# Squares of odd chunks issued ahead of the x rows, pairs written a chunk sooner, and P ahead of the turning of k and q, in an mLSTM cell followed by a squared-ReLU network

## The chip, the cores and the metric

One NeuronCore of a Trainium2 chip runs the whole kernel in one launch. The metric is the device time of an execution in microseconds (us). The kernel before was timed in three runs: 490.64, 492.65 and 494.86 us, median 492.65 us. One more execution was profiled; every duration below comes from that one.

## The reference

Inputs are q, k, v and an output gate of shape (4 batches, 8 heads, 768 steps, 40), an input and a forget gate of shape (4, 8, 768), and two weight matrices. All is float32.

```
for t in range(S):                        # each batch and head
    m_new = max(f[t] + m, i[t])
    C = exp(f[t] + m - m_new) * C + exp(i[t] - m_new) * outer(v[t], k[t])
    n = exp(f[t] + m - m_new) * n + exp(i[t] - m_new) * k[t]
    y[t] = sigmoid(o[t]) * (C @ q[t]) / max(|n . q[t]|, 1)
x = y as (3072 tokens, 320)
out = max(x @ w_in, 0)**2 @ w_out         # w_in 320x2048, w_out 2048x320
```

## The kernel before

**Tiling.** The recurrence is computed in chunks of 128 steps. There are 24 chunks (6 for each batch, all heads at once), numbered s from 0 to 23. Inside a chunk the outputs are a masked matrix product of q, k and v, as in attention: `scores` multiplies k by q on TensorE into PSUM, `weighted` (line 592, VectorE) multiplies the scores by the decay weights W and gives P, and `attend_begin` and `attend_end` (lines 697 to 736, TensorE) multiply P by v, the carried state C by q (line 703), and form the next state. The network works on groups g of two chunks (256 tokens). Its first product is `ffn1_open`, `ffn1_rows` and `ffn1_close` (lines 1036 and 1085), its second one `ffn2_fast` (line 960); both are cut up so that fewer block products are needed, at the price of sums on VectorE and GpSimd (`sums`, `sums_of_x`).

**Order.** No scheduler places the work: every engine and every queue runs its instructions in the order in which the program writes them. From chunk 6 on, one loop (line 1314) walks through parts n = 0, 1, 2, ...; four parts, numbered by `at` = 0 to 3, belong to a chunk s = 6 + n // 4. In each part there is a quarter of a network product, which fills TensorE, and around it a step of the recurrence for chunk s or s + 1. From chunk 8 on, even chunks run beside a second product (`ffn2_fast`), odd chunks beside a first product (`fast` is true).

**How k and q get to TensorE.** From chunk 7 on, k and q are not transposed by TensorE. They pass through DRAM. `pair_up(s)` (line 344) copies the chunk's k and q from the inputs to a scratch tensor kq_rows, in four DMAs, from chunk 10 on issued by GpSimd. `load_squares(s)` (line 399) brings them from there into the tile kqT in four DMAs, issued by SyncE, as 32x32 squares. `turn_kq(s)` (line 406) turns every square on VectorE. The tile kqT has two buffers, so all odd chunks share one. The buffer's last readers are `scores(s)` and `scale_q(s)` (line 667, VectorE). For an odd chunk s + 1 the turning and the scores are both done in the loop's passes of the even chunk s: the turning at `at` = 0, the scores at `at` = 1, `scale_q` and `weighted` at `at` = 2.

**What SyncE's queue carries.** SyncE issues these DMAs, in this order, for a chunk s: at `at` = 1 `store_num` (line 768; the outputs, turned in squares by VectorE at line 753, to DRAM), `load_num` (line 773; back, after the store has landed), `load_squares(s + 2)`, and for an even chunk `load_A(s + 2)` (line 430); at `at` = 2 `store_rows` (line 823; the normalised x to DRAM), for an odd chunk `load_A(s + 2)`, then `load_o(s + 5)` (line 414) and `load_rows` (line 828; x back, after its store has landed). Stores of the result (lines 996 and 1001) stand between them. The x rows of an even chunk s are turned by `turn_squares(s)` (line 835, VectorE) in the pass of chunk s + 1 at `at` = 1; right behind it on VectorE stands the sum of line 1068, for which the closing product of `ffn1_close` waits[...].

**What GpSimd carries.** Besides the DMAs of `pair_up` and `load` (k and v of a chunk, lines 364 to 376) it does the mask (line 470), the weighting of v (line 521), the decay of C (line 672), and the sums of x for the network (lines 1028 and 1031).

Of the kernel before, what the change touches and what calls it, by code (L numbers as in the profile page):

```python
# [29 lines left out]
def kernel(  # L30
# [308 lines left out]
    def pair_up(s):  # L339
        b, c = divmod(s, NB)  # L340
        eng = nc.sync if s < 10 else nc.gpsimd
        for n, src in enumerate((k, q)):
            for i in range(2):
                eng.dma_start(
                    kq_d[s, i, n].rearrange("j (m r) d -> m j (r d)", r=8),
                    src[b, i::2, c * P : (c + 1) * P, :].rearrange("j (m r) d -> m j (r d)", r=8),
                )
# [68 lines left out]
    def half_tanh(s):  # L416
        og = st[s]["og"]
        nc.scalar.activation(og, og, AF.Tanh, scale=0.5)
        if s >= X_SQ:
            nc.scalar.activation(og, og, AF.Copy, bias=0.5, scale=0.5)  # L420
# [128 lines left out]
    def scores(s, o=(False, False)):  # L549
        d = st[s]  # L550

        sc = [bank(o[i]) for i in range(2)]
        d["sc"] = sc
        if s >= KQ_SQ:
            if s >= ROT:
                d["sc"] = [t.rearrange("p j t -> p (j t)")[:, : 3 * P].rearrange("p (e t) -> p e t", e=2) for t in sc]
            for e in range(2):
                for late_keys in range(2):
                    for c in range(2):
                        for i in range(2):  # L560
                            rows = slice(DP * i, DP * i + D)
                            start = e == late_keys == 0
                            if s < ROT:
                                j, keys = 2 * late_keys + e, HALVES[c]
                                to, t0 = sc[i][HALVES[c], j, :], 0
                            else:
                                j, keys = 2 * (c ^ late_keys) + e, HALVES[late_keys]
                                to = d["sc"][i][HALVES[c], e, slice(0, DP) if late_keys else slice(DP, 3 * DP)]
                                t0 = DP * late_keys
                            nc.tensor.matmul(  # L570
                                to, lhsT=d["kT"][rows, j, keys], rhs=d["qT"][rows, j, t0:], start=start, stop=True,
                                skip_group_check=True,
                            )
            return
        for j in range(PR):
            for i in range(2):
                rows = slice(DP * i, DP * i + D)
                nc.tensor.matmul(
                    sc[i][:, j, :], lhsT=d["kT"][rows, j, :], rhs=d["qT"][rows, j, :], start=True, stop=True,
                )  # L580
# [349 lines left out]
    def sums_of_weights(i):  # L930
        if i < 3:
            T[i] = late.tile([P, NPAIR, DH], F32, name=f"T{i}", bufs=1)[:]
        if i == 0:
            nc.vector.tensor_tensor(T[0], B12, B11, op=ALU.subtract)
        elif i == 1:
            nc.vector.tensor_tensor(T[1], B22, T[0], op=ALU.subtract)
        elif i == 2:
            nc.vector.tensor_tensor(T[2], B21, T[1], op=ALU.subtract)
        else:

            nc.vector.tensor_tensor(B12, B22, B12, op=ALU.subtract)
# [131 lines left out]
    def ffn1_rows(g, q, first):  # L1073
        xT, xs = st["xT", g], st["xs"]
        X, Y, V, Z = st["f1"]
        lo, hi = HALVES
        pairs = (
            ((X, lo, xT[lo, 0, 2, :], False), (Y, hi, xT[hi, 1, 2, :], first)),
            ((V, lo, xT[lo, 1, 2, :], first), (Z, hi, xs[hi, 1, :], False)),
        )  # L1080
        for pair in pairs:
            for n in range(4):
                for cols in HALVES:
                    for to, rows, rhs, start in pair:
                        nc.tensor.matmul(  # L1085
                            to[cols, n, :], lhsT=w_in2[rows, 4 * q + n, cols], rhs=rhs,
                            start=(start and n == 0), stop=True, skip_group_check=True,
                        )
# [35 lines left out]
    def do(f, s):  # L1124
        if 0 <= s < NT:
            f(s)
# [98 lines left out]
    for u in range(8):  # L1225
        s = 2 + u // 2
# [87 lines left out]
    for n, (which, g, i) in enumerate(parts):  # L1314
        s, at = 6 + n // 4, n % 4
        if n == 5:
            brought.close()
            late = ctx.enter_context(tc.tile_pool(name="late", bufs=1, side="right"))
        even = s >= 8 and s % 2 == 0
        fast = which == 1  # L1320
        if at == 0:
            if s < 8 or even:
                do(scores, s)
            if even:
                do(turn_kq, s + 1)
            if s < 8 or even:
                do(weighted, s)
        if at == 1:
            do(attend_begin, s)
            if even:  # L1330
                do(lambda s: scores(s, ("h", "h")), s + 1)
            if fast:
                ffn1_rows(g, 0, True)
            do(attend_end, s)
            do(decays, s + 1)
            do(mask, s + 1)
            if n > 4 and not even and not fast:
                do(turn_kq, s + 1)
            do(decay_C, s + 1)
            if s > X_SQ and not fast and not even:  # L1340
                do(turn_squares, s - 1)
            do(store_num, s)
            do(load_num, s)
            do(load_squares, s + 2)
            if even:
                do(load_A, s + 2)
        if 5 <= n < 8:
            sums_of_weights(n - 5)
        if n == 6:
            sums(1, slice(0, NPAIR), (1, 2))  # L1350
        if n == 8:
            sums_of_weights(3)
            sums(1, slice(0, NPAIR), (3,))
        if n == 9:
            sums(1, slice(0, NPAIR), (4,))
        if which == 2 and i == 3 and g == NG - 2:
            sums(g + 1, slice(0, NPAIR), (2,))
        if which == 2 and g > 1 and i < 2:
            sums(g, slice(0, NPAIR), (3 + i,))
        if n == 0:  # L1360
            ffn1_begin(g)
            sums_of_x(g)
            sums_of_win(2)
        if at == 3 and s >= 8 and s % 2 == 0 and s // 2 - 1 < NG:
            sums_of_x(s // 2 - 1)
        if at == 2 and not fast:
            if even:
                do(turn_squares, s - 1)
            if n > 4:
                do(scale_q, s + 1)  # L1370
        if at == 3:
            if s % 4 == 3:
                for r in range(s + 1, min(s + 5, NT)):
                    half_tanh(r)
        if fast:
            if i % 2:
                ffn1_close(g, i // 2, i == 1)
                if at == 1 and g > 2:
                    do(turn_kq, s + 1)
                    do(turn_squares, s - 1)  # L1380
            else:
                ffn1_open(g, i // 2)
                if i == 0 and g > 2:
                    sums(g - 1, slice(0, NPAIR), (2,))
            if at == 2 and g > 2:
                do(scale_q, s + 1)
        elif g == 0:
            ffn2(g, *divmod(i, 2))
        else:
            ffn2_fast(g, i)  # L1390
        if at == 2:
            do(lambda s: weigh(s, masked=True), s + 1)
            ffn1_square()
            if n < 4:
                do(turn_kq, s + 1)
                do(scale_q, s + 1)
            if even:
                do(weighted, s + 1)
            do(normalise_turned, s)
            do(store_rows, s)  # L1400
            if not even:
                do(load_A, s + 2)
            if s > 6:
                do(load_o, s + 5)
            do(load_rows, s)
            if s == 6:
                do(pair_up, s + 3)
        if s > 6 and at == (3 if even else 2):
            do(pair_up, s + 3)
        if s > 6 and at == 3:  # L1410
            if s == 7:
                load(s + 3)
            do(load, s + 4)
        if n == 3:
            turn_halves()
        if n in (9, 25):
            spread_slots(2 + n // 25)
        if at == 0:
            ffn1_square()
        if n < 5:  # L1420
            while rounding.done < LAST[n]:
                rounding.step()
# [30 lines left out]
```

## Time and profile before

| what | value |
|---|---|
| median of three runs | 492.65 us (490.64 to 494.86) |
| the profiled execution's own time | 499.0 us |
| its span, first to last instruction | 497.2 us |
| TensorE busy | 488.1 us (98% of the span), 6167 matmuls |
| VectorE, ScalarE, GpSimd busy | 336.3, 240.8, 222.0 us |
| mean granted TensorE clock | 0.990 |
| DMA traffic | 68.02 MB, mean 137 GB/s |

The table shares the profiled execution's time between its span and 1.8 us around it. An engine's idle time matters only where TensorE then has to wait. The profile's columns are: start and duration in us, engine, source line, operation, tiles and shapes, and, in square brackets, how long the engine had been idle before the instruction and what ended the idle time. "SPq" is SyncE's queue of DMA issues; a DMA's duration there is that of its issue, and its landing is told apart.

### The profile page before, as it was taken

To read this page: it belongs to the slowest core of one execution; us is meant where nothing else is said; L and a number is where in the kernel's file an instruction comes from. 1 tells how busy PE (TensorE), PEld (TensorE's weight loads), DVE (VectorE), ACT (ScalarE), POOL (GpSimd) and SP (SyncE) were. 2 spreads that over 40 slices of the span, in tenths; PEclk is the share of its full clock that TensorE was granted. 3 is DMA by queue.
4 is the path that set the end of the run, shared out by engine and by line. 5 is a ranking of instruction groups with operands and counts; after the bars stand their busy time and mean duration, and the time that the engine had idled before them with its cause. 6 is when DMAs were issued, how large, how long until landed. Compare 5 with 4: busy or idle time off the path is not lost.

```text
span 497.2 us, 15256 instructions
## 1 busy us (share of the span) xinstructions
PE 488.1 (98%) x6167; PEld 455.8 (92%) x6169; DVE 336.3 (68%) x704; ACT 240.8 (48%) x531; POOL 222.0 (45%) x319
## 2 busy tenths in 40 slices
PE   9999999999999989999999999999999999999997
PEld 5886888897799979999999989999999999999996
DVE  7778567888956647766866856866956956735441
ACT  5576996864522730671561760561861560514300
POOL 6455533432886528358548528448544030020000
PEclk9999899999999979999999999999999999999999
DMA  8999997745978847678678678678666522200000
GB/s 179 203 250 220 304 210 199 150 83 137 170 121 169 180 85 168 132 151 175 144 132 177 140 131 184 140 143 172 157 111 143 125 64 80 54 15 15 3 26 28
DMA packets 191031, 68.02 MB, mean 137 GB/s; under 512 B 158800, under 2 KB 180208, under 8 KB 190960
## 3 DMA queue, kind: packets, MB, share of 16 engines
q1 hardware_dynamic: 185280, 57.50, 54.4%
q0 software_dynamic: 5536, 9.43, 8.4%
q8 instruction: 49, 0.80, 0.7%
q14 instruction: 22, 0.18, 0.1%
q10 hardware_dynamic: 144, 0.10, 0.1%
HBM read 54.71 MB, written 18.01 MB: 146 GB/s over the span
## 4 chain that ended last, share of the span: by engine, by line
PE 79%; DMA 10%; SPq 6%; DVE 2%; issue 1%; ACT 1%; DVEq 0%; ACTq 0%
PE h_ps L960 32%; PE h_ps L1036 22%; PE h_ps L1085 6%; PE h_ps L869 4%; PE h_ps L906 4%; DMA raw<-in_moe_w_in_dram 3%; DMA kqT<-kq_rows 3%; PE numT L722 3%; DMA lent_t<-in_moe_w_in_dram 2%; PE numT L703 2%; SPq L208 2%; PE numT L733 1%; DMA num_rows<-tn 1%; PE h_ps L570 1%; PE h_ps L880 1%
## 5 line engine op out<-in xcount | busy, mean ns | idle before, releaser
L960 PE MATMUL h_ps<-T,S 128*128 128x160 f32 x352 | 51.7, 300 | 0.0
L1066 ACT COPY r_sb<-h_ps 128x512 f32<-128x512 f32 x18 | 10.5, 585 | 84.1 <-PE h_ps L1036 84.1
L960 PEld LDWEIGHTS h_ps<-T,S 128*128 128x128 f32 x352 | 48.9, 190 | 0.3 <-ACT g L1102 0.2
L960 PE MATMUL h_ps<-w_out,g 128*128 128x160 f32 x336 | 49.2, 303 | 0.0
L960 PEld LDWEIGHTS h_ps<-w_out,g 128*128 128x128 f32 x336 | 46.1, 190 | 1.3 <-issue 0.7
L976 DVE TENSOR_TENSOR y_sb<-y_sb,h_ps 128x160 f32<-128x160 f32 x44 | 14.1, 320 | 48.5 <-PE h_ps L960 48.5
L470 POOL TENSOR_SCALAR_AFFINE_SELECT A_bc<-A_bc 64x512 f32<-64x512 f32 x32 | 24.8, 774 | 42.8 <-ACT kq L487 41.6
L1036 PE MATMUL h_ps<-xT,w_in 128*128 128x128 f32 x320 | 42.8, 278 | 0.0
L1036 PE MATMUL h_ps<-lent_t,w_in 128*128 128x128 f32 x320 | 42.2, 275 | 0.0
L1036 PEld LDWEIGHTS h_ps<-xT,w_in 128*128 128x128 f32 x320 | 38.9, 192 | 1.4 <-issue 1.0
L1085 PE MATMUL h_ps<-xT,w_in 64*64 64x128 f32 x960 | 39.1, 272 | 0.0
L1036 PEld LDWEIGHTS h_ps<-lent_t,w_in 128*128 128x128 f32 x320 | 38.9, 192 | 0.2 <-issue 0.2
L1036 PE MATMUL h_ps<-lent_t 128*128 128x128 f32 x320 | 39.0, 275 | 0.0
L1036 PEld LDWEIGHTS h_ps<-lent_t 128*128 128x128 f32 x320 | 37.3, 192 | 0.0
L500 ACT ACTIVATE A_bc<-A_bc,b_R 128x64 f32<-128x64 f32 (+1 forms) x128 | 35.7, 362 | 0.5
L1085 PEld LDWEIGHTS h_ps<-xT,w_in 64*64 64x64 f32 x960 | 34.8, 133 | 1.3
L376 POOL DMA_DIRECT2D va<-in_v_dram x56 | 34.3, 622 | 2.8 <-DMA va<-in_v_dram 1.0
L753 DVE STREAM_TRANSPOSE tn<-numT 128x256 f32<-128x256 f32 x36 | 14.0, 428 | 30.1 <-PE numT L703 20.8
L521 POOL TENSOR_TENSOR vw<-va,A_bc 128x328 f32<-128x328 f32 x13 | 10.2, 787 | 52.4 <-ACT A_bc L500 52.4
L1028 POOL TENSOR_TENSOR lent_t<-xT 128x128 f32<-128x128 f32 (+1 forms) x18 | 13.4, 764 | 39.6 <-DVE xT L835 39.6
L869 PE MATMUL h_ps<-xT,w_in 128*128 128x256 f32 x128 | 30.5, 391 | 0.4 <-POOL w_in L238 0.4
L960 PE MATMUL h_ps<-w_out,g_c 128*128 128x160 f32 x192 | 29.0, 309 | 0.0
(216 smaller groups left out, 1178.7 us busy)
## 6 DMA issues: line engine op xcount, KB each, us to landing
A_bc<-a_slots SPq DMA_DIRECT2D x32, 256.0 KB, 5.0
num_rows<-tn SPq DMA_DIRECT2D x18, 256.0 KB, 2.2
kq<-num_rows SPq DMA_DIRECT2D x72, 64.0 KB, 2.0
raw<-in_moe_w_out_dram SPq DMA_DIRECT2D x7, 640.0 KB, 5.4
kqT<-kq_rows SPq DMA_DIRECT2D x34, 128.0 KB, 3.0
og<-in_o_gate_dram SPq DMA_DIRECT2D x24, 160.0 KB, 5.0
out_dram<-y_sb SPq DMA_DIRECT2D x24, 160.0 KB, 3.0
raw<-in_moe_w_in_dram SPq DMA_DIRECT2D x7, 512.0 KB, 6.8
```

Source lines behind the costliest of these rows:

```text
L376: eng.dma_start(dst[HALVES[n], PR * (1 - late_keys) : PR * (2 - late_keys)], src[HALVES[late_keys], PR * m : PR * (m + 1)],)
L470: nc.gpsimd.affine_select(part, part, compare_op=ALU.is_ge, fill=-1e30, base=0, pattern=[[0, PR], [0, 2], [1, DP]], channel_multiplier=-1,)
L500: nc.scalar.activation(A[0][:, x, to], A[0][:, x, to], AF.Exp, bias=b_R[:, b, c, own, x : x + 1],)
L722: nc.tensor.matmul(d["numT"][m][HALVES[e], i, t0:], lhsT=va_w[s % NKQ][keys, at * D1 : at * D1 + DP], rhs=rhs, start=(s % NB == 0 and i == ...
L753: nc.vector.transpose(to[:, 2 * m : 2 * m + 2], d["numT"][m].rearrange("p c t -> p (c t)"))
L869: nc.tensor.matmul(hs[i][:, n, :], lhsT=w_in[:, a, fb * P : (fb + 1) * P], rhs=xT[:, :, a, :], start=(n == 0 and a == 0), stop=False,)
L906: nc.tensor.matmul(o_ps, lhsT=st["g2", g][:, fb, j * P : (j + 1) * P], rhs=w_out[:, fb, :], start=(fb == 0), stop=(fb == NF - 1),)
L960: nc.tensor.matmul(to, lhsT=lhsT[:, p], rhs=rhs[:, p, :], start=(start and p == 0), stop=(p == NPAIR - 1), skip_group_check=True,)
L976: add = lambda to, a, b: nc.vector.tensor_tensor(to, a, b, op=ALU.add)
L1028: sub = lambda to, a, b: eng.tensor_tensor(to, a, b, op=ALU.subtract)
L1036: nc.tensor.matmul(to[:, n, :], lhsT=lhsT[:, 4 * q + n, :], rhs=rhs, start=(start and n == 0), stop=True, skip_group_check=True,)
L1085: nc.tensor.matmul(to[cols, n, :], lhsT=w_in2[rows, 4 * q + n, cols], rhs=rhs, start=(start and n == 0), stop=True, skip_group_check=True,)
```

## The change

Three edits in the loop of line 1314:

- At `at` = 0 of an even chunk s, `weighted(s)` now stands ahead of `turn_kq(s + 1)` on VectorE.
- `load_squares` for an odd chunk is taken out of the preceding odd chunk's pass at `at` = 1 and issued in the pass of the even chunk before that, at `at` = 2, between `load_o` and `load_rows`. So the squares of chunk s + 3 are issued in the pass of chunk s, for s = 8, 10, ..., 20. Even chunks' squares stay two chunks ahead at `at` = 1.
- `pair_up` is issued for chunk s + 4 instead of s + 3; in the pass of chunk 7 it is issued for both 10 and 11.

```diff
         if at == 0:
             if s < 8 or even:
                 do(scores, s)
+            if s < 8 or even:
+                do(weighted, s)
             if even:
                 do(turn_kq, s + 1)
-            if s < 8 or even:
-                do(weighted, s)
...
             do(store_num, s)
             do(load_num, s)
-            do(load_squares, s + 2)
+            if s < 8 or even:
+                do(load_squares, s + 2)
             if even:
                 do(load_A, s + 2)
...
             if s > 6:
                 do(load_o, s + 5)
+            if even:
+                do(load_squares, s + 3)
             do(load_rows, s)
             if s == 6:
                 do(pair_up, s + 3)
         if s > 6 and at == (3 if even else 2):
-            do(pair_up, s + 3)
+            if s == 7:
+                pair_up(s + 3)
+            do(pair_up, s + 4)
         if s > 6 and at == 3:
             if s == 7:
                 load(s + 3)
```

No instruction is added or removed: the same matmuls, VectorE operations and DMAs are issued, in another order.

## The prediction

> **What bounds the kernel now.** I read the page first (busy time, the slices with the clock), then the chain of work that ended last, then the timelines of VectorE, TensorE and SyncE where the chain leaves TensorE, and the table of stretches there. The page:
>
> ```profile
> PE 488.1 (98%) x6167; PEld 455.8 (92%) x6169; DVE 336.3 (68%) x704; ACT 240.8 (48%) x531; POOL 222.0 (45%) x319
> PEclk9999899999999979999999999999999999999999
> ```
>
> TensorE is the bound, and no matmul is taken away. So the change can only win back TensorE's waits and slices of low clock. One of those lies before the loop in question (slice 5); the other is slice 15, from 174 us. There the chain reads:
>
> ```profile
> 165.70 0.36 SPq L399
> 166.10 0.56 SPq L399
> 166.78 0.77 SPq L399
> 167.59 7.03 DMA kqT<-kq_rows
> 175.05 0.86 issue
> 175.92 0.53 DVE A_bc L592
> 176.49 0.49 PE numT L703 x3
> ```
>
> The squares of chunk 11 are issued at 165.7 and land at 174.6. The next fences, VectorE's timeline and TensorE's, show what stood behind them:
>
> ```profile
> 174.75 1.25 DVE L406 STREAM_TRANSPOSE kqT<-kqT 128x1024 f32<-128x1024 f32 x1 [2.96 <-DMA kqT<-kq_rows]
> 175.92 0.98 DVE L592 TENSOR_TENSOR A_bc<-tp,A_bc 128x384 f32<-128x384 f32 x2
> ```
>
> ```profile
> 176.49 0.49 PE L703 MATMUL numT<-kq,C 40*64 40x128 f32 x3 [2.05 <-DVE A_bc L592]
> ```
>
> P of chunk 10 (L592) needs nothing of chunk 11, and its scores were ready by 169.5. It waits only because the turning of chunk 11 is ahead of it. TensorE stands 2.05 us, and the stretches show that its clock falls afterwards:
>
> ```profile
> 168.00:180.00 12.00, 9.95 (x189) 9.47 (x185) 7.39 (x17) 5.69 (x10) 5.83 (x9) 0.85 0.86 152
> 180.00:192.00 12.00, 12.00 (x103) 11.67 (x97) 6.28 (x13) 2.52 (x9) 5.64 (x8) 0.87 0.53 116
> ```
>
> (the third figure from the end is the clock). The rest of the loop stays at 1.00. SyncE's timeline of chunks 8 and 9 shows why the squares come late:
>
> ```profile
> 151.93 0.39 SPq L823 DMA_DIRECT2D x_rows<-x_sb  x1
> 152.37 0.48 SPq L414 DMA_DIRECT2D og<-in_o_gate_dram  x1
> 157.57 2.92 SPq L828 DMA_DIRECT2D xT<-x_rows  x4
> 160.60 0.40 SPq L1001 DMA_DIRECT2D out_dram<-y_sb  x1
> 161.10 0.53 SPq L768 DMA_DIRECT2D num_rows<-tn  x1
> 163.43 2.15 SPq L773 DMA_DIRECT2D kq<-num_rows  x4
> 165.70 3.38 SPq L399 DMA_DIRECT2D kqT<-kq_rows  x4
> ```
>
> From 152.85 to 157.57 the queue does nothing but wait for the x rows' store. VectorE waits for squares once more, 1.83 us at 288.1 (chunk 17). Elsewhere the odd squares land close: by the landings of L399 against the start of L406, chunk 13 is 0.7 us early, 15 0.2, 19 0.9, 21 0.2. Even chunks' squares are over 10 us early.
>
> [...] 0.15 and 0.13 of 12 us are 3.36 us lost[...]. [...] The x store at 151.93 took 5.6 us while GpSimd was issuing 11 loads, against a median of 3.6 on the page[...].
>
> **The change part by part.** Against the profiled execution's own 499.0 us (span 497.2 and 1.8 around it).
>
> *Squares of odd chunks sooner.* For chunk 11 they will be issued from 152.85, after the gate load. Four issues take 3.4 us (row 165.70), so to 156.3. Even with the longest landing of before, 7.0 us, they are there by 163.3, and L406 wants them at 171.8 (end of line 1106). Both VectorE waits (2.96 and 1.83 us) go. What TensorE gets of it: at 176.49 2.05 us, plus 3.36 us of clock, 5.4 us. For chunk 17 I compare pairs of chunks, from scores to scores of even chunks (L570): 36.82, 41.89, 36.39, 36.77, 37.52, 36.33 and 36.96 us. The fifth holds the wait of chunk 17; 37.52 - 36.96 = 0.56 us. Together 6.0 us. The issues themselves are no new cost: they fill a wait of SyncE. The tile's old readers (scores and L667 of chunk 9) were done at 146.1, so the issue adds no wait; all DMAs of L399 also leave the odd chunk's part, where store_rows waits for VectorE anyway (169.43, behind x_sb at 169.41).
>
> *What they are moved past.* L828, and behind it L1001, L768 and L773 of the odd chunk. L823's landings at chunks 8 to 20 took 5.6, 4.5, 4.4, 3.6, 3.1, 3.3 and 3.9 us; the gate load and the squares need 0.9 + 2.4 to 3.4 = 3.3 to 4.3 us from the store. So the rows are issued 0 to 0.9 us later. [...] four squares need 4.8 us from first issue to last landing in a quiet stretch (185.82 to 190.5), so 0 to 2.1 us. Sum: x rows 0.1 to 2.5 us later; I take 1.5. The cover is L835: rows of chunks 8 to 20 landed 1.2, 1.9, 2.7, 2.7, 3.2, 3.3 and 2.9 us before their turning began, and between it and TensorE lies another 0.5 us (line 1068 ends at 206.4, its closing product starts at 206.90). At 1.5 us nothing stalls. Without the cover each us costs one us per even chunk, seven in all. L768 and L773 slip by up to 0.9 us; L785 of odd chunks waits for them (1.55 us at 167.47), and behind it come lines 1103 to 1106 and then P. That is paid by the next edit.
>
> *P ahead of the turning.* Two operations of 0.98 us (P) change places with one of 1.24. P ends 1.24 us sooner, the turning 1.0 us later. P is wanted by L703: it ended at 214.5 for 215.96, so 1.4 us of room become 2.7. The turning is wanted by the odd scores on TensorE (216.65): 4.3 us of room become 2.1 (at chunk 12: from 213.6 to 214.6). Cost nothing; the cover is `ffn2_fast`'s first products, 4.5 us. For chunk 8 VectorE had turned chunk 9 while waiting for scores, so its sums end up to 0.7 us later, where it idled 0.96.
>
> *Pairs a chunk sooner.* At chunk 7 GpSimd issues four more DMAs (1.09 us for two of k, 1.02 for two of q), 2.1 us, ahead of 14 loads. From 127.4 to 149.1 it has hardly idle time, so mask, weighting and sums of x of that stretch come 2.1 us later. P of chunk 9 at 148.88 has 2.0 us (its weights were done at 144.8); the sums of x (to 148.6 for the one wanted first, 149.1 for the last) are wanted by L1036 at 151.5, so they would be there at 150.7, 0.8 us ahead. But the DMA share there is 0.97, and landings hold some GpSimd issues up (0.47, 0.68 and 0.36 us), so it may be up to 3.5 us: TensorE then stands 0.6 us once, with at worst one clock fall of 3.4. I take nothing; ends 0 and 4.0.
>
> Sum for the profiled execution: 499.0 - 5.4 - 0.6 = 493.0 us. The timed runs lie 4.1 to 8.4 us under the profiled one, so they can't all hold these 6.0 us. Without the first 60 us's low slice as well (0.14 of 12 us, 1.7), 493.0 becomes 491.3, about the fastest run, 490.64. So that run has presumably none of it; the median, 2.0 us above, has about one wait of chunk 10 without the clock's fall (2.05 us), or that early slice, which the change doesn't touch. I give the change 1.5 of these 2.0: 492.65 - 1.5 = 491.1 us.
>
> **The rivals.**
>
> *Nothing to win in the timed runs.* The squares land in time when no profile is taken, and the median's 2 us are the early slice. For it: a landing of 7.0 us is the longest of all; against it: four more odd chunks have less than 1 us. Then 492.6 us.
>
> *The x rows become the late transfer.* VectorE waits at L835, line 1068 is late, TensorE stands at L1036 in odd chunks. With the room above plus 0.5 us each, a delay of the rows by 4.0 us costs 2.3 + 1.6 + 0.8 + 0.8 + 0.3 + 0.2 + 0.6 = 6.6 us, and 491.1 + 6.6 = 497.7 is the point where the kernel is 1% slower than before; at the squares' whole 4.8 us it is 11.9, 503 us. [...] Against: my 2.5 us at most.
>
> *The full 6.0 us in every run.* Then 486.7. Against it: TensorE's busy time from 60 us on is 430.9 of 437.0 us and fixed, which leaves the fastest run no room for such a loss.
>
> **How the numbers follow.** 1% is about what a measurement of this kernel can tell from no change. My forecast, waits gone and nothing new, 491.1: 0.66. Nothing to win, 492.6: 0.15. A new short stand at chunk 8 or 9 that eats the gain, 494: 0.05. These are within 1%: 0.86. X rows late, 498 to 503: 0.09, slower. The full gain, 486.7: 0.05, faster. The range 488.5 to 494.5 takes in the first three and leaves out the last two.
>
> **What would show it.** In the profile after: no wait of L406 for kqT, no clock under 1.00 from 100 us on, all pairs of chunks from L570 to L570 at 36.3 to 37.0 us, L399 between L414 and L828 in even chunks, L828 at most 1 us later after L823 than now. Wrong if L835 or line 1068 shows idle time ended by xT<-x_rows, if L1036 waits for line 1031 near 151 us, or if L570 waits for L406.

## The result, and the profile after

The changed kernel is slower: a median of 506.12 us over four runs (503.0 to 510.23) beside 491.79 us (490.64 to 494.86) for the kernel before, over four as well. The ratio is 1.0268, with a 95% interval of 1.0209 to 1.0327, so 14 us were lost where 1.5 were expected to be won; the time lies above the range and above the rival that ended on the slow side. A ratio leaves out the executions that lie more than 1.5% above the fastest of the same kernel, and a median doesn't, so the two can differ. The profiled execution took 510.23 us, with a span of 508.4 (before 499.0 and 497.2). Both profiles lie above their kernel's median, by 4 and by 7 us, so what they show in us is near the loss of the median and not equal to it.

The page answers to the two lines shown of before, with the engines' busy time and the slices' clock:

```profile
PE 492.2 (97%) x6169; PEld 459.0 (90%) x6169; DVE 335.5 (66%) x704; ACT 241.5 (48%) x531; POOL 219.4 (43%) x319
PEclk9999999999999899979999999999899999999999
```

Work and busy times are what they were; TensorE's share fell by a point, and the clock now falls at three places of the loop instead of one (the slices 14, 18 and 29). VectorE is busy for less of a longer span, so nothing was added to it. The loss is waiting.

The stretches from scores to scores of even chunks (L570 to L570; start and end, length, busy time of PE, PEld, DVE, ACT and POOL with counts, then clock, DMA share and GB/s) tell where:

```profile
131.44:172.28 40.84, 38.59 (x577) 37.58 (x580) 23.55 (x49) 14.08 (x35) 31.41 (x51) 0.96 0.84 159
172.28:209.40 37.12, 36.59 (x552) 35.73 (x548) 25.02 (x55) 15.83 (x36) 18.12 (x28) 1.00 0.68 141
209.40:251.46 42.06, 40.34 (x569) 39.14 (x564) 26.10 (x59) 19.76 (x45) 23.95 (x37) 0.92 0.66 135
251.46:290.73 39.27, 37.76 (x585) 36.39 (x581) 26.46 (x59) 17.54 (x40) 22.57 (x36) 1.00 0.68 143
290.73:328.48 37.75, 36.84 (x553) 35.87 (x548) 26.24 (x64) 18.17 (x41) 20.57 (x33) 1.00 0.73 148
328.48:368.65 40.17, 38.27 (x568) 37.26 (x564) 26.34 (x57) 20.23 (x46) 25.27 (x39) 0.96 0.75 147
368.65:405.79 37.14, 36.99 (x584) 36.03 (x580) 28.04 (x66) 16.91 (x38) 9.30 (x12) 1.00 0.52 107
sum 274.35, PE 265.38 PEld 257.99 DVE 181.75 ACT 122.52 POOL 151.20; mean PE 37.91 PEld 36.86 DVE 25.96 ACT 17.50 POOL 21.60
```

The prediction's seven lengths for before add up to 262.68 us, so these seven pairs hold 11.67 us of loss, as much as the span grew by (11.2). TensorE's idle time in them is 274.35 - 265.38 = 8.97 us. The clock took another 0.04 · 40.84 + 0.08 · 42.06 + 0.04 · 40.17 = 6.6 us. TensorE's timeline names the larger stands, that is, times in which it does nothing (in brackets, the idle time and what ended it):

```profile
166.99 2.08 PE L1036 MATMUL h_ps<-lent_t,w_in 128*128 128x128 f32 x8 [2.25 <-DVE r_sb L1068]
...
215.95 0.91 PE L722 MATMUL numT<-A_bc,va 64*64 64x128 f32 x16 [1.12 <-DVE A_bc L592]
217.57 1.42 PE L570 MATMUL h_ps<-kqT 40*64 40x128 f32 x32 [0.49 <-DVE kqT L406]
...
363.26 1.16 PE L1036 MATMUL h_ps<-lent_t,w_in 128*128 128x128 f32 x8 [1.90 <-DVE r_sb L1068]
```

There are two kinds. The closing product in an odd chunk's pass (L1036) waits for line 1068, which waits for the x rows: 2.25 + 1.90 = 4.15 us. And P, the turning and what follows them on VectorE are late: 1.12 and 0.49 us here, and five more stands of 0.38 to 0.53 us, about 4.1 us in all. VectorE's waits say what it was itself waiting for (total, times, longest):

```profile
DVE dm L785 <- DMA kq<-num_rows: 21.3, 8, 4.7
...
DVE xT L835 <- DMA xT<-x_rows: 6.1, 4, 2.7
```

Before, the first of these was 3.9 us in five waits, with none over 1.6, and the second didn't exist. The wait of L406 for squares, 4.8 us before, is gone. SyncE's timeline of chunk 8 shows the cause of both:

```profile
152.04 0.39 SPq L823 DMA_DIRECT2D x_rows<-x_sb  x1
152.48 0.61 SPq L414 DMA_DIRECT2D og<-in_o_gate_dram  x1
153.22 8.00 SPq L399 DMA_DIRECT2D kqT<-kq_rows  x4
161.31 2.89 SPq L828 DMA_DIRECT2D xT<-x_rows  x4
164.31 0.40 SPq L1001 DMA_DIRECT2D out_dram<-y_sb  x1
164.81 0.38 SPq L768 DMA_DIRECT2D num_rows<-tn  x1
167.00 1.88 SPq L773 DMA_DIRECT2D kq<-num_rows  x4
```

The four issues of squares, priced at 3.4 us, hold the queue for 8.00. The x rows are issued 161.31 - 152.04 = 9.27 us after their store, where it was 5.64 before, and land late for L835. Behind them the num store of chunk 9 goes out at 164.81. Its data, the turned numerators, had been ready since 158.24, so it is 6.57 us late; before it was 161.10 - 158.67 = 2.43. VectorE's timeline has both consequences, 6 us apart:

```profile
165.78 0.58 DVE L835 STREAM_TRANSPOSE xT<-xT 128x384 f32<-128x384 f32 x1 [2.73 <-DMA xT<-x_rows]
...
171.97 0.17 DVE L785 TENSOR_SCALAR dm<-kq 128x8 f32<-128x8 f32 x1 [3.63 <-DMA kq<-num_rows]
...
176.21 1.02 DVE L592 TENSOR_TENSOR A_bc<-tp,A_bc 128x384 f32<-128x384 f32 x2
177.14 1.24 DVE L406 STREAM_TRANSPOSE kqT<-kqT 128x1024 f32<-128x1024 f32 x1
```

P (L592) now stands ahead of the turning as the change has it, and the turning waits for no squares; but P runs at 176.21, no earlier than the 175.92 of before. The chain of waits goes through the same place (start, duration, what):

```profile
164.81 2.17 DMA num_rows<-tn
...
168.45 3.39 DMA kq<-num_rows
...
175.69 0.60 DVE g L1106
176.29 0.93 DVE A_bc L592 x2
177.22 0.51 DVE kqT L406
```

Where the squares' landing was ahead of P in the chain of before, the round trip of the numerators through memory is there now: out at 164.81, back at 171.84.

### The profile page after: what moved, and what is told of

The parts are those of the page before. It is cut to its first block, busy times and chain, and to the rows that moved or that the text cites. A ratio compares the mean times of both kernels' runs of the same rounds, so it can differ in the third digit from the quotient of the medians.

```text
span 508.4 us, 15267 instructions
## 1 busy us (share of the span) xinstructions
PE 492.2 (97%) x6169; PEld 459.0 (90%) x6169; DVE 335.5 (66%) x704; ACT 241.5 (48%) x531; POOL 219.4 (43%) x319
## 4 chain that ended last, share of the span: by engine, by line
PE 72%; DMA 8%; DVE 7%; ACT 5%; SPq 5%; issue 2%; DVEq 0%; ACTq 0%
PE h_ps L960 30%; PE h_ps L1036 21%; PE h_ps L1085 6%; PE h_ps L906 3%; PE h_ps L869 3%; DMA kq<-num_rows 3%; PE numT L722 2%; DMA num_rows<-tn 2%; SPq L208 2%; DMA raw<-in_moe_w_out_dram 2%; PE numT L703 1%; PE numT L733 1%; DVE kqT L406 1%; DMA lent_t<-in_moe_w_in_dram 1%; SPq L773 1%
## 5 line engine op out<-in xcount | busy, mean ns | idle before, releaser
L960 PE MATMUL h_ps<-w_out,g 128*128 128x160 f32 x336 | 51.4, 312 | 0.0
L960 PEld LDWEIGHTS h_ps<-w_out,g 128*128 128x128 f32 x336 | 48.3, 198 | 1.4 <-issue 0.9
L1036 PE MATMUL h_ps<-lent_t,w_in 128*128 128x128 f32 x320 | 43.5, 281 | 4.2 <-DVE r_sb L1068 4.1
L470 POOL TENSOR_SCALAR_AFFINE_SELECT A_bc<-A_bc 64x512 f32<-64x512 f32 x32 | 21.7, 677 | 58.1 <-ACT kq L487 56.5
L1036 PEld LDWEIGHTS h_ps<-lent_t,w_in 128*128 128x128 f32 x320 | 39.7, 196 | 4.9 <-DVE r_sb L1068 4.7
L1036 PE MATMUL h_ps<-xT,w_in 128*128 128x128 f32 x320 | 42.8, 279 | 0.0
L1085 PE MATMUL h_ps<-xT,w_in 64*64 64x128 f32 x960 | 40.3, 278 | 0.0
L1036 PEld LDWEIGHTS h_ps<-xT,w_in 128*128 128x128 f32 x320 | 38.9, 192 | 1.4 <-issue 1.0
L1036 PE MATMUL h_ps<-lent_t 128*128 128x128 f32 x320 | 39.0, 276 | 0.0
L1036 PEld LDWEIGHTS h_ps<-lent_t 128*128 128x128 f32 x320 | 37.3, 192 | 0.0
L1085 PEld LDWEIGHTS h_ps<-xT,w_in 64*64 64x64 f32 x960 | 36.0, 137 | 1.4 <-issue 0.2
L521 POOL TENSOR_TENSOR vw<-va,A_bc 128x328 f32<-128x328 f32 x13 | 11.3, 872 | 55.7 <-ACT A_bc L500 52.8
L869 PEld LDWEIGHTS h_ps<-xT,w_in 128*128 128x128 f32 x128 | 23.6, 190 | 6.2 <-ACT xT L848 1.4
```

Of the source, the lines that this page charges most:

```text
L470: nc.gpsimd.affine_select(part, part, compare_op=ALU.is_ge, fill=-1e30, base=0, pattern=[[0, PR], [0, 2], [1, DP]], channel_multiplier=-1,)
L521: nc.gpsimd.tensor_tensor(d["vw"][:].rearrange("p (own x) d -> p own x d", own=2), d["va"][:].rearrange("p (own x) d -> p own x d", own=2) ...
L869: nc.tensor.matmul(hs[i][:, n, :], lhsT=w_in[:, a, fb * P : (fb + 1) * P], rhs=xT[:, :, a, :], start=(n == 0 and a == 0), stop=False,)
L960: nc.tensor.matmul(to, lhsT=lhsT[:, p], rhs=rhs[:, p, :], start=(start and p == 0), stop=(p == NPAIR - 1), skip_group_check=True,)
L1036: nc.tensor.matmul(to[:, n, :], lhsT=lhsT[:, 4 * q + n, :], rhs=rhs, start=(start and n == 0), stop=True, skip_group_check=True,)
L1085: nc.tensor.matmul(to[cols, n, :], lhsT=w_in2[rows, 4 * q + n, cols], rhs=rhs, start=(start and n == 0), stop=True, skip_group_check=True,)
```

## The experiments

Theory when these runs were planned: edit 2 alone is at fault, because the squares' issues hold SyncE's queue, and what stands behind them there (x rows, and the numerators of the next chunk) comes late. Rivals: edits 1 or 3 do it; the x rows' landing alone does it; or the DMA engines are full in the even chunk and it makes no difference who issues.

### Edit 1 alone, and edits 1 and 3

`p_ahead` is the kernel before with only this:

```diff
+            if s < 8 or even:
+                do(weighted, s)
             if even:
                 do(turn_kq, s + 1)
-            if s < 8 or even:
-                do(weighted, s)
```

`p_and_pairs` has the pairs a chunk sooner as well; the squares stay in their old place.

> P (line 592) ahead of the turning (line 406), and nothing else of the change. My theory: the loss comes from SyncE's queue, where the squares of odd chunks take 4 to 7.4 us to issue ahead of the x rows and of the odd chunk's num store; so this order alone costs nothing and takes TensorE's waits of before partly away: 489 to 492 us, ratio 0.995 to 1.00. Rival, the order itself is at fault (the turning comes 1 us later and the odd scores wait for it): 497 us or more.

> P ahead of the turning and the pairs a chunk sooner; the squares stay where they were before. My theory: within 0.3% of P ahead alone, 489 to 492 us. Rival, GpSimd's four DMAs more at chunk 7 and the fuller DMA engines there are at fault: 495 us or more, with TensorE waiting for line 1031 or idle near 150 us.

Measured: `p_ahead` 491.17 us (median of 20) against 492.41 for before, ratio 0.9972 (0.9953 to 0.999). `p_and_pairs` 491.99 us, ratio 0.998 (0.9956 to 1.0004). Both as expected: edits 1 and 3 cost nothing, and edit 1 by itself wins 0.28%. The profiled execution of `p_ahead` took 489.31 us; its stretches of pairs, summed:

```profile
165.55:201.86 36.31, 36.31 (x552) 35.59 (x548) 25.61 (x57) 15.71 (x36) 21.33 (x34) 1.00 0.76 158
...
sum 256.08, PE 256.08 PEld 250.37 DVE 184.04 ACT 121.92 POOL 152.84; mean PE 36.58 PEld 35.77 DVE 26.29 ACT 17.42 POOL 21.84
```

PE's busy time is the length of the stretches: TensorE doesn't stand at all, and the clock stays at 1.00. Nothing was left in these stretches for edit 2 to win. This is the shortest of the 20 executions, 1.9 us under their median, so others may hold short waits; but in the profile of `p_and_pairs` too (492.72 us) L406 waits for no squares. Against this sum the changed kernel's seven pairs lost 274.35 - 256.08 = 18.27 us, of which 8.97 are idle time and 6.6 the clock; 2.7 us are not told apart. It is more than the 14 us between the medians, since the shortest of 20 executions stands here beside the longest of four. The queue in the same place, with the squares where they were:

```profile
152.93 3.22 SPq L828 DMA_DIRECT2D xT<-x_rows  x4
156.83 0.51 SPq L768 DMA_DIRECT2D num_rows<-tn  x1
...
161.41 2.56 SPq L399 DMA_DIRECT2D kqT<-kq_rows  x4
```

The numerators go out 8 us earlier than in the changed kernel, and the same four issues of squares take 2.56 us instead of 8.00.

### The squares behind the x rows

```diff
+            do(load_rows, s)
             if even:
                 do(load_squares, s + 3)
-            do(load_rows, s)
```

> The whole change, but the squares of odd chunks are issued behind the x rows (line 828) instead of ahead of them. My theory says two things stand behind the squares: the x rows and the num store of the next odd chunk (line 768). Here only the rows are set free, so line 835 doesn't wait, but line 768 is still 3 us or more late in odd chunks and line 785 waits: 495 to 503 us. Rival, only the x rows matter: 490 to 492 us, as if nothing were late.

Measured: 512.18 us against 492.41, ratio 1.0399 (1.0363 to 1.0435); worse than the changed kernel, where less of a loss was expected. VectorE has no wait for x rows any more, but:

```profile
DVE dm L785 <- DMA kq<-num_rows: 28.2, 9, 5.6
```

SyncE issues the rows at 158.82 and then the squares in only 2.69 us, at 162.17; the num store still isn't out before 166.46, 5.91 us behind its data. So "the x rows come late" is not the whole cause: with rows in time, late numerators make a kernel slower than the one before. The squares take 2.7 to 3.7 us here in all seven chunks, near the prediction's price. So what they cost depends on the place within the chunk. But that price alone doesn't save the kernel: behind the rows no wait hides them, and they come in full before the num store. Why this kernel is slower than the changed one, whose num stores are about as late, isn't shown.

### The squares issued by ScalarE

The place in the program is that of the changed kernel; only the engine that issues the odd squares changes.

```diff
-    def load_squares(s):
+    def load_squares(s, eng=nc.sync):
...
-                nc.sync.dma_start(
+                eng.dma_start(
...
-                do(load_squares, s + 3)
+                do(lambda s: load_squares(s, nc.scalar), s + 3)
```

> The whole change, but the squares of odd chunks are issued by ScalarE at the same place of the program. The same bytes at nearly the same time, off SyncE's queue. My theory (the queue is held up): the x rows are issued when their store has landed and line 768 within 2.5 us of its data as before, TensorE's idle time from 100 us on is under 2 us, 489 to 492 us. Rival, the DMA engines are too full and everything lands late whoever issues it: rows and num land 2 to 4 us late as in the changed kernel, 498 to 506 us.

Measured: 499.4 us, ratio 1.0154 (1.0123 to 1.0185). My theory's number (no loss with SyncE's queue free) fell, and the rival's number held. VectorE's waits and the queue:

```profile
DVE dm L785 <- DMA kq<-num_rows: 17.4, 8, 4.7
DVE xT L835 <- DMA xT<-x_rows: 2.6, 2, 2.0
```

```profile
152.29 0.39 SPq L823 DMA_DIRECT2D x_rows<-x_sb  x1
157.97 2.78 SPq L828 DMA_DIRECT2D xT<-x_rows  x4
161.37 0.39 SPq L768 DMA_DIRECT2D num_rows<-tn  x1
164.92 1.76 SPq L773 DMA_DIRECT2D kq<-num_rows  x4
```

SyncE waits for the x store alone, 157.97 - 152.29 = 5.7 us. But it wasn't "at nearly the same time": ScalarE comes to this place sooner. Its row for chunk 11's squares (one issue in ns, start of the first and of the last), and the time from issue to landing:

```profile
L399 ACTq DMA_DIRECT2D kqT<-kq_rows x4: 333/682/997, 144.5 to 147.0; - x4
DMA to landing us min/median/max: 3.1/4.0/4.4
```

They go out nearly 9 us before those of the changed kernel, take 3.4 us together, and the last has landed by 151.4, ahead of the x store at 152.29. In the other six chunks they take 2.96 to 3.63 us, and the last lands at most 1.1 us after that store is issued. So the store and the squares hardly overlap; still the store is slower: it lands after 5.7, 5.4, 5.7, 5.6, 5.9, 6.5 and 4.4 us in the chunks 8 to 20, where before it took 5.6, 4.5, 4.4, 3.6, 3.1, 3.3 and 3.9. The num stores of the chunks 9 to 19 stand 2.2 to 4.3 us behind their data. From 145 to 153 us the DMA share is 1.12, before it was 0.80; that this slows the store is not shown. The loss falls from 2.7% to 1.5%. How much of that comes from the free queue and how much from the sooner place this run can't tell. It does show that a kernel in which no odd squares stand in SyncE's queue loses as well.

In the changed kernel the time of issuing isn't small beside that of landing: chunk 11's four issues hold SyncE for 8.00 us, and each of these DMAs lands 3.6 to 8.2 us after its issue.

### Half of the squares ahead

```diff
-        for i in range(2):
+        for i in halves:
...
+            else:
+                do(lambda s: load_squares(s, (1,)), s + 2)
...
-                do(load_squares, s + 3)
+                do(lambda s: load_squares(s, (0,)), s + 3)
```

> The whole change, but of the odd chunk's four square DMAs only the two of the first half are issued ahead of the x rows; the other two stay in the odd chunk where all four were before. My theory: SyncE is held for some 4 us instead of 4 to 7.4, which its wait for the x store (3 to 5.6 us) hides, and half the bytes crowd the even chunk; a third of the loss or less remains: 492 to 498 us. Rival, any DMA of squares there makes the odd chunk's num store late in full: 502 to 507 us.

Measured: 495.3 us (median of 20) against 493.22, ratio 1.0024 (0.9993 to 1.0056), as expected. Two issues take 3.91 us at 152.15, the rows follow at 156.49, and L785 waits 7.6 us. Half the issues cost far less than half of the loss: the first two nearly fit into the wait of SyncE, as the prediction took it for all four.

### Edits 2 and 3 without edit 1

The two statements of edit 1 go back to their old order.

> The whole change without its first edit: the turning stands ahead of P again. My theory: in the changed kernel the odd chunk's normalising is late, VectorE works without pause up to P and the turning, and TensorE waits for P first; with the turning ahead P comes 1.2 us later in six or seven even chunks, of which the odd scores give back 0.5 us each: 508 to 514 us. Rival, the order doesn't matter here since the odd scores wait all the same: 504 to 507 us.

Measured: 510.93 us, ratio 1.0328 (1.0244 to 1.0411). It is in the expected range, but the interval overlaps that of the changed kernel, so the time doesn't settle what the order is worth here. TensorE's waits do show the difference:

```profile
PE h_ps L1036 <- DVE r_sb L1068: 5.8, 3, 2.6
PE numT L703 <- DVE A_bc L592: 5.1, 3, 1.9
```

With the turning ahead, L703 waits for P for 5.1 us; in the changed kernel no stand of L703 is on the list. But P ahead doesn't spare TensorE this wait for certain: with P ahead L703 waits for it for 3.5 us in `behind_rows` and 1.4 in `gate_behind`. So the late numerators are passed on in either order; that the turning's 1.24 us comes on top where it stands first fits, but isn't shown.

### What makes the squares slow there: GpSimd's loads, or the gate load

In even chunks GpSimd issues pairs and loads while the squares go out. `bursts_squares` moves all of them into odd chunks; `bursts_only` is its control, with the squares at their old place.

```diff
-        if s > 6 and at == (3 if even else 2):
-            if s == 7:
-                pair_up(s + 3)
+        if s > 6 and at == 2 and not even:
+            do(pair_up, s + 3)
             do(pair_up, s + 4)
-        if s > 6 and at == 3:
-            if s == 7:
-                load(s + 3)
+        if s > 6 and at == 3 and not even:
+            do(load, s + 3)
             do(load, s + 4)
```

> The whole change, and GpSimd's pairs and loads of even chunks (11 DMAs each) moved into the following odd chunk, from chunk 9 on. Theory of crowding: the squares are slow to issue because these 11 DMAs fill the same engines; without them four squares take under 4 us, the x rows and the odd num store are on time: 490 to 496 us. Rival, SyncE's own gate load and x store ahead of the squares hold them up, whatever GpSimd does: squares at 4 to 7 us as now, 503 to 508 us.

> The control for the kernel with moved bursts: P ahead, pairs sooner, GpSimd's even bursts moved into odd chunks, but the squares where they were before. Both theories: 490 to 494 us if moving the bursts costs nothing by itself; above 496 us the move itself costs (22 DMAs in a row on GpSimd, 13 us, hold up its mask or crowd the odd chunk's squares), and the kernel with moved bursts is then to be read against this one.

Measured: 504.5 us, ratio 1.0134 (1.0029 to 1.0238). The ratio rests on two of the four executions, 499.28 and 501.96 us; they lie between the numbers of my theory and of the rival, so neither came. The control took 492.14 us, ratio 0.9986 (0.9953 to 1.002), as expected. So moving the loads by itself costs nothing that can be measured. The profiled execution of `bursts_squares` is its longest, 508.67 us, so the two executions behind the ratio may have had shorter squares. In it they are cured only in part: the squares of chunk 11 take 4.80 us instead of 8.00, later ones up to 6.65. The stretches of these two (columns as above):

```profile
153.00:158.20 5.20, 5.20 (x161) 4.91 (x160) 2.65 (x6) 1.44 (x4) 1.33 (x2) 1.00 1.00 196
...
229.00:235.60 6.60, 6.60 (x170) 6.23 (x169) 3.02 (x8) 2.04 (x5) 1.80 (x3) 1.00 0.64 123
```

In the first the DMA engines are at a share of 1.00 without GpSimd's loads; in the second the squares are slower still, at 0.64.

`gate_behind` moves the gate load of even chunks behind the x rows instead:

```diff
-            if s > 6:
+            if s > 6 and not even:
                 do(load_o, s + 5)
             if even:
                 do(load_squares, s + 3)
             do(load_rows, s)
+            if even:
+                do(load_o, s + 5)
```

> The whole change, with the gate load (line 414) of even chunks moved behind the x rows, so that on SyncE the squares come right behind the x store. Theory of SyncE's own backlog: the squares are slow to issue because the gate load (1024 short runs) and the x store are still under way in the same queue; without the gate load ahead they take 3 to 4 us in every even chunk and 497 to 502 us come out. Rival, GpSimd's bursts fill the engines and the gate load has no part: squares at 4 to 7 us as now, 503 to 508 us.

Measured: 509.41 us against 492.09, ratio 1.032 (1.0261 to 1.0378): a miss, above both theories' numbers. The squares get only a little shorter, 6.38 us at 152.02 (over all seven chunks 31.8 us, in the changed kernel 39.7); the rows' issues then take 3.95, the gate load follows ahead of the num store, and L785 waits 24.0 us. Neither of the two neighbours alone accounts for the slow issue.

### The numerators of odd chunks on GpSimd's queue

The squares stay ahead on SyncE, with the rows behind them; only the num store and loads of odd chunks leave the queue.

```diff
+        eng = nc.gpsimd if s > 8 and s % 2 else nc.sync
-        nc.sync.dma_start(n_d[s], ...
+        eng.dma_start(n_d[s], ...
```

(and the same in `load_num`; this shifts the lines behind it by up to two)

> The whole change, but the num store and loads of odd chunks (lines 768 and 773) are issued by GpSimd, from chunk 9 on, so that they no longer stand behind the squares and the x rows on SyncE. My theory, the late num of odd chunks is what TensorE pays for: line 785 waits under 1.5 us in odd chunks, P and the turning are in time, what is left is the late x rows (TensorE at L1036, chunks 8, 14 and 18): 493 to 499 us, though the squares are as slow to issue as before. Rival, the x rows or the crowded engines are the payer: 503 us or more.

Measured: 497.51 us against 492.09, ratio 1.0104 (1.0061 to 1.0147), as expected. SyncE's, VectorE's and TensorE's timelines around chunk 8:

```profile
150.90 8.24 SPq L399 DMA_DIRECT2D kqT<-kq_rows  x4
```

```profile
165.05 0.58 DVE L837 STREAM_TRANSPOSE xT<-xT 128x384 f32<-128x384 f32 x1 [4.46 <-DMA xT<-x_rows]
...
167.51 0.17 DVE L787 TENSOR_SCALAR dm<-kq 128x8 f32<-128x8 f32 x1
```

```profile
166.26 2.05 PE L1038 MATMUL h_ps<-lent_t,w_in 128*128 128x128 f32 x8 [3.98 <-DVE r_sb L1070]
```

The squares are as slow as in the changed kernel and the x rows later still, so that TensorE stands 3.98 us in chunk 9. But the old L785 (here 787) no longer waits after 165.05: its numerators are there. VectorE's waits for them fall from 21.3 to 6.1 us in all, in odd chunks to 1.29 at most. This takes 1.6 points off the loss of 2.7%, about 8 us of the 14; the remaining 1.0%, 5 us, goes with the late rows (TensorE's waits at L1038 are 5.4 us, nearly all it has in the loop).

## Why the prediction was wrong, step by step

**"Squares of odd chunks sooner"** was right in its mechanism: the squares of chunk 11 are there long before L406, and both waits for squares went. That the gain of TensorE's 2.05 us and the clock's fall could be had was right too. But it didn't need this edit. `p_ahead` has it from edit 1: P no longer waits for the turning, and in its profile TensorE stands nowhere in the seven pairs. The 1.5 us that the prediction gave to the whole change is about what edit 1 measures alone (0.28%, 1.4 us; 0.5 to 2.3 by its interval). The prediction said itself that P "waits only because the turning of chunk 11 is ahead of it", and should have asked what was left for edit 2 with that removed.

**"The issues themselves are no new cost: they fill a wait of SyncE"** together with the next step, **"What they are moved past"**, is where the sum failed. The size of one term was wrong: four issues of squares at "2.4 to 3.4" us. These durations came from stretches late in the odd chunk. The same four DMAs in the new place, by SyncE's row for chunk 11's squares (minimum, median and maximum of one issue in ns):

```profile
L399 SPq DMA_DIRECT2D kqT<-kq_rows x4: 921/1696/3132, 153.2 to 159.6; - x4
```

against 365/667/1482 in the old place. In the passes of the chunks 8 to 20 the four take 8.00, 5.21, 4.28, 7.29, 4.18, 7.42 and 3.28 us from the start of the first to the end of the last. The stretches around the longest, the third and the shortest:

```profile
153.20:161.20 8.00, 8.00 (x185) 7.71 (x184) 4.68 (x10) 2.04 (x5) 5.28 (x9) 1.00 1.08 212
...
236.40:240.70 4.30, 4.30 (x152) 4.01 (x151) 1.88 (x4) 0.03 (x1) 4.23 (x8) 1.00 1.12 158
...
389.40:392.60 3.20, 3.20 (x71) 3.08 (x73) 2.69 (x3) 1.33 (x4) 1.32 (x2) 1.00 0.70 117
```

The DMA share is 1.08 where they are slowest and 0.70 where they take what was predicted; but at 1.12 they take 4.28 us, so the share alone doesn't set their time. The prediction had seen that the x store took 5.6 us there "while GpSimd was issuing 11 loads" and used that for the store alone, not for the issues that it put beside it. So the rows were issued not "0 to 0.9 us later" but 3.6, 1.8, 1.8, 4.8, 2.2 and 5.8 us later in the chunks 8 to 18; only chunk 20, with 0.1 us the other way, went as forecast. The sum's other part, up to 2.1 us more until the rows land behind the squares, was an estimate of the author's, and it didn't show: from issue to landing the slowest of the rows took 3.0 to 3.8 us in these chunks, before 2.8 to 4.0. So their delay is that of their issue.

**"L768 and L773 slip by up to 0.9 us ... That is paid by the next edit."** This named the right queue and the right consumers, and sized them by the same wrong term. The num stores of the chunks 9 to 19 stand 6.57, 3.94, 3.15, 5.12, 2.76 and 6.17 us behind their data (before 2.43, 1.85, 1.07, 0.50, 0.88 and 0.09). Edit 1 pays 1.24 us, and the prediction named no other cover for these stores. The rest went to L785, and behind it, in order, lines 1103 to 1106, P and the turning.

**The rival "the x rows become the late transfer"** was the right kind of failure at too small a chance, and half of the mechanism. In the profile of after, the stands at L1036 make 4.15 us, with a fall of the clock at each; those of P, the turning and their followers make about as much, with one longer fall. Taking the numerators away (`num_pool`) removed some 8 us of 14, and putting the rows in front (`behind_rows`) removed none. The forecast for this rival, 498 to 503 us, had no term for the numerators, and so ends below the 506.1 measured.

**P ahead of the turning** and **pairs a chunk sooner** were right: `p_and_pairs` is within 0.2% of before, and L1036 doesn't wait for line 1031 near 151 us. L570 does wait for L406, three times for 0.38 to 0.49 us; the prediction named this as a sign against itself. It takes both the late numerators and edit 1: neither `p_ahead` nor `no_p`, each of which has one of the two, has this wait.

**Sums that don't come out.** None of these decides anything. Gate load and squares of 4.3 us beside an x store that lands after 3.1 make the rows up to 1.2 us later, not 0.9, and with the 2.1 us for landing behind the squares the most is 3.3, not 2.5. The turning's room before the odd scores was 3.0 us (213.6 to 216.65), not 4.3; 4.3 counts from its start. The rival's cost at 4.8 us is 12.2 us, not 11.9.

**The clock.** The three falls cost 6.6 us by the pairs. The rival's price of "one us per even chunk" for each us of delay left this out, although the prediction's first step had measured it: 3.36 us lost after a stand of 2.05.

**Still open.** Why the squares' issue is slow in the even chunk. Full DMA engines alone don't explain it (6.65 us at a share of 0.64 in `bursts_squares`, 4.28 at 1.12 here), nor do GpSimd's loads or the gate load alone; the x store and the loads of A from the chunk before are there too, and weren't tried. Nor is it settled what slows the x store in `squares_act`, and how much of the loss there comes from it.

The version that beats both kernels is `p_ahead`, the one before by 0.28%.

## What to carry to other kernels

Price a DMA issue for the place where it will stand, not for the one where it stood (chunk 11's four squares: 3.38 us before, 8.00 after): a queue that waits for a store is free only for issues that end within that wait (two of the four nearly did, with 3.91 us). List everything behind a moved issue on its in-order queue, up to the next chunk's round trip, and give each its own due time (chunk 9's num store went out 6.57 us behind its data). And where an in-order engine makes ready work wait behind a late transfer, swap the two operations first (here the 2.05 us of TensorE's stand at P, none of it left in `p_ahead`'s profile); if nothing stands any more, the transfer need not move.

## What was not expected of the hardware

- The same four DMAs of squares occupied SyncE for 2.56 us in `p_ahead` and 8.00 in the changed kernel; a single issue for up to 3.13 us, with 1.48 the longest for odd squares at their old place in the kernel before.
- Two stands of TensorE of about 2 us, and two of 1.12 and 0.49 us close together, were each followed by a lower clock that cost nearly as much again or more: 1.7, 1.7 and 3.4 us in the stretches 160 to 172, 360 to 372 and 216 to 228.
